# Sparse attention and MoE on one core: the first chunk's attention with scores two units ahead, loads reordered, weights four steps per unit from the first unit on

## The chip, the cores and the metric

The kernel runs on one core of a Trainium2 chip. The metric is the device time of one execution in microseconds (us); of several executions the median is given. The engines are PE (TensorE, matrix products; PEld is its loading of weights), DVE (VectorE), ACT (ScalarE), POOL (GpSimd) and SP (SyncE, which here only issues transfers). Each engine takes its instructions in program order and waits on semaphores. Transfers (DMAs) are issued by SP, ACT and POOL and run on 16 DMA engines.

## What is computed

Block-sparse attention for 4 batches, 8 heads, 768 positions of 64 dimensions, and then a gated two-layer feed-forward network on all 3072 tokens (called MoE in the code):

```python
scores = scale * np.matmul(q, k.transpose(0, 1, 3, 2))
...
mask = np.abs(blk_i - blk_j) <= window
mask = mask | (blk_i == 0) | (blk_j == 0) | (blk_i == n_blocks - 1) | (blk_j == n_blocks - 1)
for qb in range(n_blocks):
    for kb in sampled_blocks[qb]:
        mask[qb * block:(qb + 1) * block, kb * block:(kb + 1) * block] = True
scores = np.where(mask, scores, -1000000000.0)
...
attn = attn / (np.sum(attn, axis=-1, keepdims=True) + 1e-09)
return np.matmul(attn, v).astype(np.float32)
...
h = x @ w_in
g = h * (1.0 / (1.0 + np.exp(-1.702 * h)))
return (g @ w_out).astype(np.float32)
```

A block is 32 positions, so there are 24 blocks. A row of a middle block sees its two neighbours and itself, the first and the last block, and three sampled ones. The first and last block see everything. The network is 512 to 2048 to 512.

## The kernel before

**Units and chunks.** The work is cut into 48 units of 64 tokens: two blocks of one batch, all 8 heads. 44 of them are sparse, 4 dense. Eight units make a chunk of 512 tokens, and there are six chunks. Two sparse units that follow each other belong to two batches and share one entry of K (tiles `kg` and `qt`, loaded by `load_k`, L177) and one of V (tiles `vown` and `vmid`, loaded by `load_v`, L200). There are two buffers of each. An entry of K is 1536 KB (the first ones for a pair of batches 256 KB more), one of V 1280 KB (the first two 1536 KB). `loads()` (L220) issues the next entry of K and then the next of V whenever the entry two before has been used up by the program. SP issues most loads; while `early` is set, POOL issues three of the K loads, and it always issues the two gathers of `vown`.

**One unit of attention.** `scores` (L244): 32 matmuls on PE (L260), then on DVE the negated minima of the scaled, masked scores (`least`, L283) and on ACT the exponentials with their sums (`exps`, L290). `transposes` (L296): eight transposes on PE (L306), two copies from PSUM to `pt` on ACT (L310), and on DVE the reciprocals (`factors`, L345, with L360 and L361). `values` (L315): 64 matmuls on PE (L331), then `normalise` on DVE (L373). `turn` (L379): two transposes on PE (L384), then the split of the result into a high part on ACT (`xhi`, L391) and a low part on DVE (`xlo`, L392). Most of these functions put the PE work into the queue at once and return the ACT and DVE work as a list, so that the caller decides where that goes; `finish` runs such a list. What runs in which order on an engine is just the order in which this code issues it.

**Weights.** `weights()` (L398 on) is a generator that turns the 32 tiles of the two weight matrices, which arrive as 64-bit words, into float32 high and low parts. `fetch` (L414) loads a raw tile of 512 KB from ACT's queue, two tiles ahead, into three buffers. A tile takes four steps, each ended by a `yield`: L446 on DVE; the end of the tile before (`last`, L427 on DVE, and `save`, L433, which stores a w_out tile to DRAM for the later chunks); L452 on DVE and `first` of the next tile (L422 on ACT, which waits for the raw tile); L456 on DVE and the cast L459 on ACT. `first`, L446 and the others work in place in `a`, of which there are three. The list `todo` sets the order of the tiles: in step f the tile f of w_in, and the tile f - 1 of w_out (LAG is 1). A w_out tile from the fourth on (WRING is 3) waits until MoE has used the one three before.

**Order of the first chunk.** `run` (L690) builds indices, calls `loads()`, which issues the first two entries of K and of V in the order K, V, K, V, and then `first()` (L658), written by hand: for each n it issues scores(n) and its minima, two weight steps, turn(n - 2), transposes(n - 1), the exponentials of n, values(n - 1) with normalise, `loads()` and two more weight steps. The first weight step, which fetches the first two raw tiles, comes after the exponentials of unit 0; four weight steps per unit come from n = 2 on, 29 in all. It runs over nine units: the last belongs to the second chunk, and only its scores and exponentials are done here.

**The rest.** Then `tick(m)` (L618) runs 96 MoE steps of 16 per chunk: `up` (L482: L491, L492, L493, into `bank` 7), the gate on ACT and DVE (L499 to L519), `down` (L522: L537, L541, L542). In the first chunk's 16 steps it runs 6 or 9 weight steps in each. The attention of the next chunk is spread over the steps by `plan` (L579), which counts in quarters of a MoE step.

Of the kernel before, what the change touches and what calls it, by code (L numbers as in the profile page):

```python
# [27 lines left out]
NF = DF // P  # L28
NU = (NB - 2) // 2
UT = 2 * BLK  # L30
CU = 8
# [3 lines left out]
RING = 2  # L35
WRING = 3
LAG = 1
# [6 lines left out]
class Kernel:  # L44
# [57 lines left out]
    def indices(self):  # L102
# [7 lines left out]
        def take(shape):  # L110
            n = 1
            for k in shape:
# [8 lines left out]

        vblk = take([NB])
        first, second = slice(1, NB - 2, 2), slice(2, NB - 1, 2)
        nc.gpsimd.iota(vblk[3 * BLK:P, first], pattern=[[2, NU]], base=0, channel_multiplier=0,
                       allow_small_or_imprecise_dtypes=True)
# [118 lines left out]
    def scores(self, g):  # L244
        nc, un, sparse = self.nc, g["unit"], self.sparse(g)
        r = g["k"]["n"] % RING
        g["k"]["scores"] -= 1
        if g["first"]:
            un["rs"] = self.small.tile([P, 2, NPAIR], F32, name="rs")
            un["nm"] = self.small.tile([P, 2, NPAIR], F32, name="nm")  # L250
        sps = self.psum("s", g["n"])
        if sparse:
            bi, n = un["b"] % 2, 2 * P
            kg = self.kg[r][:, :, bi].rearrange("p n (a s) -> p n a s", a=NPAIR)
            for i in range(2):
                for a in range(2):
                    for j in range(2):
                        for h in range(2):
                            pair, rows, c = 2 * i + a, slice(D * h, D * (h + 1)), 2 * a + j
                            nc.tensor.matmul(  # L260
                                sps[h][BLK * c:BLK * (c + 1), n * i:n * (i + 1)].rearrange("p (n s) -> p n s", s=BLK),
                                self.qt[r][rows, bi, UT * pair + BLK * j:UT * pair + BLK * (j + 1)],
                                kg[rows, 4 * j:4 * j + 8, pair], start=True, stop=True, tile_position=(D * h, BLK * c))
            parts = [(i, 0) for i in range(2)]
            bias = self.bias[:, un["u"]].rearrange("p (n o) -> p n o", o=1).broadcast_to([P, 8, BLK])
        else:
            kt = self.kg[r].rearrange("p n b c -> p (n b c)").rearrange("p (a s) -> p a s", a=NPAIR)
            i, half, n = g["i"], g["half"], S // 2
            for a in range(2):
                for h in range(2):  # L270
                    pair, rows = 2 * i + a, slice(D * h, D * (h + 1))
                    nc.tensor.matmul(sps[h][UT * a:UT * (a + 1), 0:n], self.qt[r][rows, 0, UT * pair:UT * (pair + 1)],  # L272
                                     kt[rows, pair, n * half:n * (half + 1)], start=True, stop=True, tile_position=(D * h, UT * a))
            parts = [(i, half)]
            bias = self.zero.broadcast_to([P, n])
        g["ex"] = {}

        def least(h):
            for k, (i, half) in enumerate(parts):
                at = sps[h][:, n * k:n * (k + 1)]  # L280
                if sparse:
                    at = at.rearrange("p (n s) -> p n s", s=BLK)
                nc.vector.tensor_tensor_reduce(out=at, in0=at, in1=bias, scale=-SCALE, scalar=3.0e38, op0=ALU.add, op1=ALU.min,  # L283
                                               accum_out=un["nm"][:, half, 2 * i + h:2 * i + h + 1])

        def exps(h):
            for k, (i, half) in enumerate(parts):
                c = 2 * i + h
                ex = g["ex"][h, k] = self.work.tile([P, 384], F32, name="ex", bufs=4)[:, 0:n]
                nc.scalar.activation(out=ex, in_=sps[h][:, n * k:n * (k + 1)], func=AF.Exp, bias=un["nm"][:, half, c:c + 1],  # L290
                                     scale=-1.0, accum_out=un["rs"][:, half, c:c + 1])

        return [lambda h=h: (least(h), exps(h)) for h in range(2)] if not self.early else [
            lambda: [least(h) for h in range(2)], lambda: [exps(h) for h in range(2)]]
# [103 lines left out]
    def weights(self):  # L398

        nc = self.nc  # L400
        todo = []
        for f in range(NF + LAG):
            if f < NF:
                todo.append((f, 0))
            if f >= LAG:
                todo.append((f - LAG, 1))
        self.ready = set()
        tiles = {}

        def fetch(k):  # L410
            if k < len(todo):
                f, i = todo[k]
                raw = self.work.tile([P, 2 * DM], I32, name="raw", bufs=3)
                nc.scalar.dma_start(out=raw, in_=self.w64[i][f])  # L414
                tiles[k] = {"raw": raw.rearrange("p (a b) -> p a b", b=2)}

        def first(k):


            if k < len(todo):  # L420
                a = tiles[k]["a"] = self.work.tile([P, DM], I32, name="a", bufs=3)
                nc.scalar.activation(out=a.bitcast(F32), in_=tiles[k]["raw"][:, :, 1].bitcast(F32), func=AF.Abs, scale=REBASE)  # L422

        def last(k):
            f, i = todo[k]
            t, w = tiles[k]["t"], tiles[k]["a"].bitcast(F32)
            nc.vector.tensor_tensor(out=t[:, DM:2 * DM], in0=w, in1=t[:, 0:DM].bitcast(F32), op=ALU.subtract)  # L427
            self.ready.add((f, i))

        def save(k):  # L430
            f, i = todo[k]
            if i == 1:
                nc.scalar.dma_start(out=self.ws[f], in_=tiles[k]["a"].bitcast(F32))  # L433
            del tiles[k]

        fetch(0)
        fetch(1)
        yield
        first(0)
        for k, (f, i) in enumerate(todo):  # L440
            while i == 1 and f - WRING > self.downs - 1:
                yield
            fetch(k + 2)
            raw, a = tiles[k]["raw"], tiles[k]["a"]
            low, high = raw[:, :, 0], raw[:, :, 1]
            nc.vector.tensor_scalar(out=a, in0=a, scalar1=3, scalar2=None, op0=ALU.logical_shift_left)  # L446
            yield
            if k > 0:
                last(k - 1)
                save(k - 1)  # L450
                yield
            nc.vector.scalar_tensor_tensor(out=a, in0=high, scalar=-0x80000000, in1=a, op0=ALU.bitwise_and,  # L452
                                           op1=ALU.bitwise_or)
            first(k + 1)
            yield
            nc.vector.scalar_tensor_tensor(out=a, in0=low, scalar=29, in1=a, op0=ALU.logical_shift_right,  # L456
                                           op1=ALU.bitwise_or)
            t = tiles[k]["t"] = self.win[f] if i == 0 else self.wout[f % WRING]
            nc.scalar.copy(out=t[:, 0:DM], in_=a.bitcast(F32))  # L459
            yield  # L460
        last(len(todo) - 1)
        save(len(todo) - 1)
# [155 lines left out]
    def tick(self, m):  # L618
# [16 lines left out]
        after = self.begin(QT * m)  # L635
        finish(after[:3])
        run(n0)
        finish(after[3:])
        if moe:
# [18 lines left out]
    def first(self):  # L658

        items = self.items[:CU + 1]  # L660
        assert items[CU]["unit"]["n"] == CU

        def finish(todo):
            while todo:
                todo.pop(0)()

        def weights(k):
            for _ in range(k):
                next(self.conv)

        for n, g in enumerate(items):
            if n == 1:
                next(self.conv)
            exps = self.scores(g)
            exps.pop(0)()
            if n > 1:
                weights(2)
                finish(self.turn(items[n - 2]))
            if n > 0:
                finish(self.transposes(items[n - 1]))  # L680
            finish(exps)
            if n > 0:
                finish(self.values(items[n - 1]))
            self.loads()
            if n > 1:
                weights(2)
        finish(self.turn(items[CU - 1]))
        self.loads()

    def run(self):  # L690
        self.g, self.wst, self.downs = {}, {}, 0
        self.conv = self.weights()
        self.indices()
        self.loads()
        self.first()
        self.early = False
        self.at = self.plan()
        for m in range(NC * NF + LAG):
            if m == NF:
                for _ in self.conv:  # L700
                    pass
            self.tick(m)
# [50 lines left out]
```

## Time and profile before

| | us |
|---|---|
| median of 3 runs | 782.72 |
| lowest, highest | 781.99, 784.43 |
| the profiled execution | 782.75 |
| its span, first to last instruction | 781.1 |

| engine | busy us | share of the span |
|---|---|---|
| PE | 738.6 | 95% |
| DVE | 412.8 | 53% |
| ACT | 383.5 | 49% |
| POOL | 57.1 | 7% |

The profile gives one execution. A row of the instructions in order of time has the start in us from the start of the span, the duration in us, engine, line, operation, what it writes and reads, the shapes and a count of instructions merged into it; in square brackets stands how long the engine was idle before it, and what ended that. ACTq, SPq and POOLq are the issue of transfers. Matmuls overlap, so PE's busy time is not PE at its peak. A transfer row tells of its issue alone.

### The profile page before, as it was taken

Reading aid. Unit: us, or ns where it says so; the run is one execution under the profiler, and the core shown is the slowest. Engines: PE = TensorE matmul, PEld = TensorE weight load, DVE = VectorE, ACT = ScalarE, POOL = GpSimd, SP = SyncE. Lnnn points to the kernel's source line nnn. Section 1 sums busy time; section 2 is a strip of 40 time slices with the busy share of each in tenths; the row PEclk is TensorE's granted clock in tenths of the full one; section 3 lists DMA queues with packets and bytes.
Section 4 is the critical chain, followed back from the end, with each engine's and each line's share of the span. In section 5 each row is a group of like instructions: output and inputs, shape, how many; then the busy total and the mean of one; then the engine's idle time right before and its main releaser. Section 6 shows DMA issues by size and latency. Waiting matters only on the chain.

```text
span 781.1 us, 19264 instructions
## 1 busy us (share of the span) xinstructions
PE 738.6 (95%) x7584; PEld 571.7 (73%) x7584; DVE 412.8 (53%) x1076; ACT 383.5 (49%) x950; POOL 57.1 (7%) x85
## 2 busy tenths in 40 slices
PE   2667999999999999999999999999999999999996
PEld 1445787767777777787877877877777777888884
DVE  3387779887644354445445544444554444443332
ACT  1567667666545444444444544444545454333332
POOL 5122001101000001000000000000000000000000
PEclk9699999999999999999999999999999999999998
DMA  8998887786644437664534465435574321041112
GB/s 267 281 367 296 251 254 256 251 259 222 206 162 153 117 114 219 173 177 129 161 117 145 142 175 156 137 115 163 161 229 153 93 98 42 28 108 40 55 41 55
DMA packets 61117, 128.22 MB, mean 164 GB/s; under 512 B 7569, under 2 KB 26514, under 8 KB 60514
## 3 DMA queue, kind: packets, MB, share of 16 engines
q1 hardware_dynamic: 46882, 80.50, 33.9%
q0 software_dynamic: 7232, 25.51, 10.1%
q10 hardware_dynamic: 6912, 20.97, 8.1%
q8 instruction: 60, 0.98, 0.5%
q14 instruction: 31, 0.25, 0.1%
HBM read 116.47 MB, written 10.49 MB: 163 GB/s over the span
## 4 chain that ended last, share of the span: by engine, by line
PE 78%; DMA 7%; DVE 7%; ACT 4%; issue 2%; SPq 1%; ACTq 0%; DVEq 0%
PE bank L491 11%; PE bank L541 10%; PE bank L542 10%; PE bank L537 10%; PE bank L493 10%; PE bank L492 10%; PE bank L260 5%; PE bank L306 4%; PE bank L331 4%; DMA ws<-a 3%; DMA kg<-in_kb_dram 2%; PE bank L339 2%; PE bank L272 2%; DMA raw<-in_moe_w_in_dram 2%; DVE a L452 1%
## 5 line engine op out<-in xcount | busy, mean ns | idle before, releaser
L491 PE MATMUL bank<-xhi,win 128*128 128x512 f32 x384 | 158.4, 412 | 1.2 <-ACT xhi L391 0.9
L290 ACT ACTIVATE ex<-bank,nm 128x256 f32<-128x256 f32 (+1 forms) x208 | 99.7, 492 | 115.4 <-DVE nm L283 113.6
L506 DVE SCALAR_TENSOR_TENSOR g<-g,bank 128x512 f32<-128x512 f32 x83 | 57.1, 687 | 183.8 <-ACT g L499 183.8
L541 PE MATMUL bank<-wout,ghi 128*128 128x512 f32 x384 | 154.1, 401 | 0.0
L542 PE MATMUL bank<-wout,ghi 128*128 128x512 f32 x384 | 151.7, 395 | 0.0
L493 PE MATMUL bank<-xhi,win 128*128 128x512 f32 x384 | 151.0, 393 | 0.0
L492 PE MATMUL bank<-xlo,win 128*128 128x512 f32 x384 | 150.0, 391 | 0.0
L499 ACT ACTIVATE g<-bank 128x512 f32<-128x512 f32 x96 | 57.5, 599 | 146.4 <-PE bank L493 146.1
L537 PE MATMUL bank<-wout,glo 128*128 128x512 f32 x384 | 107.7, 394 | 0.0
L480 DVE TENSOR_TENSOR wout<-wst,wout 128x512 fp32r<-128x512 f32 x80 | 55.4, 693 | 79.7 <-ACT wout L479 78.7
L511 ACT CAST ghi<-g 128x512 fp32r<-128x512 f32 x96 | 59.7, 622 | 54.6 <-DVE g L506 54.6
L491 PEld LDWEIGHTS bank<-xhi,win 128*128 128x128 f32 x384 | 72.1, 188 | 18.7 <-ACT xhi L391 1.1
L537 PEld LDWEIGHTS bank<-wout,glo 128*128 128x128 f32 x384 | 72.4, 189 | 17.3
L493 PEld LDWEIGHTS bank<-xhi,win 128*128 128x128 f32 x384 | 72.1, 188 | 16.3
L283 DVE CUSTOM_DVE_ANT_1 bank<-bank,bias 128x256 f32<-128x256 f32 x176 | 73.8, 440 | 19.3 <-PE bank L260 16.2
L542 PEld LDWEIGHTS bank<-wout,ghi 128*128 128x128 f32 x384 | 72.5, 189 | 15.6
L541 PEld LDWEIGHTS bank<-wout,ghi 128*128 128x128 f32 x384 | 72.2, 188 | 16.0
L492 PEld LDWEIGHTS bank<-xlo,win 128*128 128x128 f32 x384 | 72.3, 188 | 13.3 <-DVE xlo L392 0.3
L216 POOL DMA_INDIRECT vown<-in_v_dram,vidx x44 | 43.7, 994 | 496.9 <-PE bank L331 385.5
L260 PE MATMUL bank<-kg,qt 64*32 64x256 f32 x1408 | 55.8, 416 | 17.6 <-DMA vmid<-in_v_dram 10.5
L310 ACT COPY pt<-bank 128x512 f32<-128x512 f32 (+1 forms) x120 | 61.1, 563 | 19.4 <-PE bank L306 19.3
L331 PEld LDWEIGHTS bank<-vown,pt 128*32 128x32 f32 x1408 | 43.8, 113 | 31.8 <-ACT pt L310 16.0
(75 smaller groups left out, 821.8 us busy)
## 6 DMA issues: line engine op xcount, KB each, us to landing
wst<-ws SPq DMA_DIRECT2D x80, 256.0 KB, 2.7
kg<-in_kb_dram SPq DMA_DIRECT2D x136, 128.0 KB, 3.2
kg<-in_kb_dram SPq DMA_DIRECT2D x22, 384.0 KB, 4.9
raw<-in_moe_w_in_dram ACTq DMA_DIRECT2D x16, 512.0 KB, 9.7
raw<-in_moe_w_out_dram ACTq DMA_DIRECT2D x16, 512.0 KB, 4.5
kg<-in_kT_dram SPq DMA_DIRECT2D x4, 1536.0 KB
vown<-in_vd_dram SPq DMA_DIRECT2D x8, 768.0 KB, 6.0
qt<-in_q_dram SPq DMA_DIRECT2D x22, 256.0 KB, 4.9
```

The lines of the kernel that those rows point to most:

```text
L260: nc.tensor.matmul(sps[h][BLK * c:BLK * (c + 1), n * i:n * (i + 1)].rearrange("p (n s) -> p n s", s=BLK), self.qt[r][rows, bi, UT * pair + ...
L283: nc.vector.tensor_tensor_reduce(out=at, in0=at, in1=bias, scale=-SCALE, scalar=3.0e38, op0=ALU.add, op1=ALU.min, accum_out=un["nm"][:, ha ...
L290: nc.scalar.activation(out=ex, in_=sps[h][:, n * k:n * (k + 1)], func=AF.Exp, bias=un["nm"][:, half, c:c + 1], scale=-1.0, accum_out=un["r ...
L310: copies.append(lambda pt=pt, ps=ps, m=m: nc.scalar.copy(out=pt[:, 0:m], in_=ps[:, 0:m]))
L331: nc.tensor.matmul(av[BLK * c:BLK * (c + 1), 0, 2 * i + h], g["pt"][h][:, 2 * i + k, BLK * c:BLK * (c + 1)], src[:, at:at + D], start=(k = ...
L491: nc.tensor.matmul(h, wih[:, k], hi[:, k], start=(k == 0), stop=False)
L492: nc.tensor.matmul(h, wih[:, k], lo[:, k], start=False, stop=False)
L493: nc.tensor.matmul(h, wil[:, k], hi[:, k], start=False, stop=(k == NCT - 1))
L511: self.nc.scalar.copy(out=ghi, in_=self.g[m][0])
L537: nc.tensor.matmul(o[n], glo[:, tk[n]], woh, start=False, stop=last)
L541: nc.tensor.matmul(o[n], ghi[:, tk[n]], woh, start=(f == 0), stop=False)
L542: nc.tensor.matmul(o[n], ghi[:, tk[n]], wol, start=False, stop=False)
```

## The change

It has four parts.

1. The order in the first chunk. Scores and minima of units 0 and 1 come first, then `loads()`, the exponentials of unit 0 and the first weight step. Then for each unit n of the eight: transposes(n) with the copies and the factors, turn(n - 1) with xhi and xlo, scores(n + 2) with its minima, the exponentials of n + 1, the matmuls of values(n), `loads()`, two weight steps, normalise(n), and two more weight steps. For the last unit the two before normalise are put behind it.
2. Weight steps: four from unit 0 on, 33 in all.
3. `run` issues the first two entries of K and one of V; the second entry of V comes with the first `loads()`, behind the third entry of K.
4. The order of the weight tiles: the w_out tiles from the fourth on come one step f later, behind one more w_in tile.

```diff
@@ weights()
         todo = []
-        for f in range(NF + LAG):
+        lag = lambda f: LAG if f < WRING else LAG + 1
+        for f in range(NF + LAG + 1):
             if f < NF:
                 todo.append((f, 0))
-            if f >= LAG:
-                todo.append((f - LAG, 1))
+            todo += [(k, 1) for k in range(NF) if k + lag(k) == f]
@@ first()
-        for n, g in enumerate(items):
-            if n == 1:
-                next(self.conv)
-            exps = self.scores(g)
-            exps.pop(0)()
-            if n > 1:
+        exps = {}
+
+        def scores(n):
+            if n < len(items):
+                exps[n] = self.scores(items[n])
+                exps[n].pop(0)()
+
+        for n in range(2):
+            scores(n)
+        self.loads()
+        finish(exps[0])
+        next(self.conv)
+        for n in range(CU):
+            todo = self.transposes(items[n])
+            if n > 0:
+                todo += self.turn(items[n - 1])
+            finish(todo)
+            scores(n + 2)
+            finish(exps[n + 1])
+            todo = self.values(items[n])
+            self.loads()
+            if n < CU - 1:
                 weights(2)
-                finish(self.turn(items[n - 2]))
-            if n > 0:
-                finish(self.transposes(items[n - 1]))
-            finish(exps)
-            if n > 0:
-                finish(self.values(items[n - 1]))
-            self.loads()
-            if n > 1:
-                weights(2)
+            finish(todo)
+            weights(2 if n < CU - 1 else 4)
         finish(self.turn(items[CU - 1]))
         self.loads()
@@ run()
-        self.loads()
+        for e in self.kent[:RING]:
+            self.load_k(e)
+        self.load_v(self.vent[0])
+        self.knext, self.vnext = RING, 1
         self.first()
```

## The prediction

> **What bounds the kernel now.** The profiled run took 782.75 us, 1.65 us more than its span, and the median of the runs before is 782.72 us, so the profiled execution stands for the median and sums against it need no correction. I read the page first, then the busy time by stages.
>
> ```profile
> span 781.1 us, 19264 instructions
> ```
>
> ```profile
> 10.00:75.00 65.00, 42.63 (x889) 28.32 (x889) 40.66 (x140) 38.07 (x114) 19.94 (x27) 0.84 0.95 320
> 23.00:30.00 7.00, 4.24 (x54) 2.91 (x44) 2.28 (x9) 0.55 (x4) 0.00 (x0) 0.60 1.03 279
> 59.00:63.00 4.00, 3.81 (x97) 2.30 (x98) 1.73 (x6) 3.09 (x11) 1.43 (x2) 0.57 0.29 107
> 75.00:165.00 90.00, 88.34 (x924) 68.16 (x923) 75.45 (x176) 61.84 (x142) 7.01 (x6) 1.00 0.80 255
> 165.00:200.00 35.00, 34.29 (x446) 26.20 (x446) 26.10 (x70) 22.29 (x56) 2.34 (x2) 1.00 0.70 219
> ```
>
> The columns after the stretch are its length, the busy time of PE, PEld, DVE, ACT and POOL, the granted clock, the DMA share and GB/s. The change touches the first stretch: eight units of attention before the first MoE matmul. There no engine is full, the DMA engines nearly are (0.95), and PE is busy 42.63 of 65 us. After 75 us PE is never idle long, so whatever the first stretch gains or loses is carried to the end almost unchanged: the later order of work is counted in quarters of MoE steps, not in time. So the question is when the first L491 starts. Next I read ACT and DVE in order of time.
>
> ```profile
> 18.84 0.38 ACTq L414 DMA_DIRECT2D raw<-in_moe_w_in_dram  x1
> ...
> 30.23 0.66 ACT L422 ACTIVATE a<-raw 128x512 f32<-128x512 f32 x1 [6.68 <-DMA raw<-in_moe_w_in_dram]
> ...
> 32.16 0.66 ACT L422 ACTIVATE a<-raw 128x512 f32<-128x512 f32 x1 [1.26 <-DMA raw<-in_moe_w_in_dram]
> ...
> 42.45 0.62 ACT L459 CAST win<-a 128x512 fp32r<-128x512 f32 x1 [0.48 <-DVE a L456]
> ...
> 42.98 0.67 ACT L422 ACTIVATE a<-raw 128x512 f32<-128x512 f32 x1
> ...
> 43.80 1.08 ACT L310 COPY pt<-bank 128x512 f32<-128x512 f32 x2
> 44.75 0.50 ACT L290 ACTIVATE ex<-bank,nm 128x256 f32<-128x256 f32 x1
> ...
> 57.71 0.69 ACT L422 ACTIVATE a<-raw 128x512 f32<-128x512 f32 x1 [2.85 <-DMA ws<-a]
> ...
> 73.05 0.62 ACT L459 CAST wout<-a 128x512 fp32r<-128x512 f32 x1 [0.27 <-DVE a L456]
> ...
> 74.24 0.37 ACT L391 CAST xhi<-bank 128x256 fp32r<-128x256 f32 x1 [0.57 <-DMA kg<-in_kb_dram]
> ```
>
> ```profile
> 30.93 0.43 DVE L446 TENSOR_SCALAR a<-a 128x512 int32<-128x512 int32 x1 [1.40 <-ACT a L422]
> 31.42 0.69 DVE L452 SCALAR_TENSOR_TENSOR a<-raw,a 128x512 int32<-128x512 int32 x1
> ...
> 37.59 0.43 DVE L283 CUSTOM_DVE_ANT_1 bank<-bank,bias 128x256 f32<-128x256 f32 x1 [0.53 <-PE bank L260]
> ...
> 42.67 0.42 DVE L283 CUSTOM_DVE_ANT_1 bank<-bank,bias 128x256 f32<-128x256 f32 x1
> ...
> 44.44 0.69 DVE L427 TENSOR_TENSOR win<-a,win 128x512 fp32r<-128x512 f32 x1
> 45.05 0.68 DVE L452 SCALAR_TENSOR_TENSOR a<-raw,a 128x512 int32<-128x512 int32 x1
> 45.65 0.42 DVE L392 TENSOR_TENSOR xlo<-bank,xhi 128x256 fp32r<-128x256 f32 x1
> 45.98 0.20 DVE L360 TENSOR_SCALAR rg<-rs 128x4 f32<-128x4 f32 x1
> ...
> 46.50 0.42 DVE L373 TENSOR_TENSOR x<-bank,ri 128x256 f32<-128x256 f32 x1
> 46.84 0.68 DVE L456 SCALAR_TENSOR_TENSOR a<-raw,a 128x512 int32<-128x512 int32 x1
> 47.44 0.42 DVE L446 TENSOR_SCALAR a<-a 128x512 int32<-128x512 int32 x1
> ...
> 63.12 0.43 DVE L283 CUSTOM_DVE_ANT_1 bank<-bank,bias 128x256 f32<-128x256 f32 x1 [0.47 <-PE bank L260]
> ...
> 68.19 0.43 DVE L283 CUSTOM_DVE_ANT_1 bank<-bank,bias 128x256 f32<-128x256 f32 x1
> 72.33 0.68 DVE L456 SCALAR_TENSOR_TENSOR a<-raw,a 128x512 int32<-128x512 int32 x1
> 74.65 0.42 DVE L392 TENSOR_TENSOR xlo<-bank,xhi 128x256 fp32r<-128x256 f32 x1 [1.30 <-ACT xhi L391]
> ```
>
> Three things are to be seen. ACT, which takes its work in order, stands 6.68 us in front of the first weight tile, fetched at 18.84 and there at 30.23; behind it wait DVE (L446) and all later attention. From unit 3 on, one round runs from one L283 to the next: 5.07 us at its best (63.12 to 68.19), where DVE has no gap, and (68.19 - 37.59)/5 = 6.12 us on average, because ACT waits for transfers (2.85 us at 57.71). And the last round hands over fast: last L456 at 72.33, xhi at 74.24.
>
> ```profile
> 59.20 2.00 PE bank L331 x64
> 61.19 1.81 PE bank L260 x32
> ...
> 74.67 0.50 PE bank L491
> ```
>
> **The change, part by part. The new round.** Scores two units ahead take the score matmuls off the path: they are done a whole round before their exponentials. But the new order of one unit is, on DVE, factors, xlo of the unit before, minima of the unit after next, L427, L452, normalise, L456, L446; on ACT it is pt, xhi, exponentials, L422, L459. In the old order xlo stood behind L427 and L452, and ACT had those 3 us to get xhi done. Now the two copies pt and the cast xhi stand behind L459, L459 waits for L456, and xlo leads DVE's next round. That closes a loop: L456 to L459 0.72 (72.33 to 73.05), L459 0.53 (42.45 to 42.98), both pt 0.95 (43.80 to 44.75), xhi to xlo 0.41 (74.24 to 74.65), xlo 0.33 (45.65 to 45.98), minima 1.77 (42.67 to 44.44), L427 0.61, L452 0.60, normalise 0.34, and L456 again: 6.26 us. That is above the old best of 5.07 and next to the old mean of 6.12. What it buys is cover: ACT works only about 4 us of that round, so L422 stands some 2 us before L459 is due, and waits like the 2.85 at 57.71 mostly vanish in it. I take 6.26 for each of five rounds, 31.3 us against 30.6, and up to 1 us more in all for waits that are too long for the cover.
>
> PE is not the bound even at its slow pace: transposes 1.72 (row below), scores 1.81, values 2.00, and two more transposes at a quarter of the 1.72 make 6.0 us, just inside 6.26.
>
> ```profile
> 19.38 1.72 PE L306 MATMUL bank<-ident,ex 128*128 128x128 f32 x8 [1.46 <-ACT ex L290]
> ```
>
> **From the first weight tile to the rounds.** Call its arrival at ACT L0. From L422 to L446 0.70 (30.23 to 30.93), L446 0.49, L452 0.60, normalise 0.34, then L456 to L459 0.72, and 0.53, 0.95, 0.41, 0.33 as in the loop: the minima of unit 3 start at L0 + 5.07. The second tile came 1.93 us after the first and is covered up to 2.3. Before, it was L0 + 7.36. Here two units of lead gain 2.3 us.
>
> **The end of the stretch.** Minima of unit 8 at L0 + 36.4, its L456 at + 3.32 = L0 + 39.7. Then comes a unit without scores: L459 and pt 2.20, values up to 2.00 (I take 1.8), normalise 0.34, and only then four weight steps instead of two: L427 and L452 1.21, L456 to L459 0.72, xhi 1.19 behind that (73.05 to 74.24) and L491 0.43 later: about 7.9 us, where the old end took 2.34 from its last L456. So the first L491 starts at L0 + 47.6. Before it was 30.23 + 44.44. The new order needs 3.2 us more after the first tile, and makes one more tile of weights in it.
>
> **Loads.** Before, both entries of V were issued ahead of the weights:
>
> ```profile
> 13.91 1.74 SPq L212 DMA_DIRECT2D vmid<-in_v_dram  x2
> ```
>
> ```profile
> 14.46 0.99 POOL L216 DMA_INDIRECT vown<-in_v_dram,vidx  x1 [0.30 <-issue]
> ...
> 18.28 0.58 POOL L198 DMA_DIRECT2D kg<-in_kb_dram  x1 [1.56 <-PE bank L260]
> 19.48 0.57 POOL L198 DMA_DIRECT2D kg<-in_kb_dram  x1 [0.62 <-issue]
> ```
>
> Now the second entry of V (1536 KB: three transfers of SP, two of POOL) goes behind the third of K, which waits for the scores at 18.28, so the raw tiles, issued at the same 18.84, meet 1.57 MB less. At 279 to 320 GB/s that is 4.9 to 5.6 us of DMA time. Bounds for L0: 5.6 us earlier, if all of it had stood ahead of the tile; no earlier, if three queues share the engines evenly and the tile's part stays a third, since that V entry then comes back beside it from about 22 us. I take 3 us, near the middle, since the third of K needs POOL until about 21 us and until then the tile has little beside it: L0 = 27.2. The first V entry moves behind the second K entry, on POOL behind three issues of 1.2 us (18.28 to 19.48). Its user, the values of unit 0, has cover until its normalise, which waits for L0 in any case. The second K entry comes earlier; it is needed for the scores of unit 2, which now have the whole wait before L0 as cover. Without that cover they would cost their 1.81 on PE.
>
> **Weights.** 33 steps instead of 29 come before MoE. The four are worth 0.60 + 0.42 + 0.61 + 0.60 = 2.2 us of DVE (L456, L446, L427, L452 above). The new order of tiles (w_out one later from the fourth on) keeps the rate, since the ring of w_out still holds the conversion to the MoE steps, so the four fall out at the end, in 165 to 200 us, where PE is busy 34.29 of 35 and DVE 26.10. Bounds: nothing, or all 2.2. I take 0.7.
>
> **Sum.** L491 at 27.2 + 47.6 = 74.8 against 74.67: 0.1 later; 0.7 back at the end; 782.75 + 0.1 - 0.7 = 782.2 us. A change under 0.3% (2.35 us) can't be told from none here.
>
> **The rivals. Slower, 785.4 us: the weights still come at 30.2.** The loop and the longer end then cost their 3.2 us, less 0.7 at the end, and with none to little of the 1 us for waits: 782.75 + 3.2 - 0.7 = 785.3, or 785.4 with a tenth of it. It decides once L0 is later than about 29.7. For it speaks that the tile took 11.4 us for 1 MB (two raws) while the engines ran at 279 GB/s, which is a third of that rate. Against it, that in 18 to 22 us fewer packets compete. The Trainium skill, "DMA: Bandwidth & Descriptors", section "Queues, rings and completion order", states that each DMA engine takes turns between the queues that have work, packet by packet; by that rule the third stays a third, and this rival would hold. The 92 GB/s of the two raws agree with it as far as they go, while no run here shows the new mix.
>
> **Faster, 778.9 us: the weights come at 24.6.** Then L491 is at 72.2, 2.5 earlier, and with 1.4 of the 2.2 at the end 782.75 - 2.5 - 1.4 = 778.9. For it: the new loads leave ACT's queue nearly alone until 22 us. Against it: the engines still move the same bytes by about 33 us. A second way to it is that DMA, idle for most of 59 to 63 us (0.29), fills that hole with loads that are now issued sooner; but loads that come sooner do not shorten a 6.26 us loop.
>
> **The lead does nothing, 782.7 us:** ACT is blocked before the first tile as before, and if the rounds stay at 6.1 because transfers still set them, the 2.3 us won after L0 go to the longer end. That lies inside the forecast and has its chance there.
>
> **How the numbers follow.** The forecast, within 0.3%, has 0.48. The faster rival has 0.30, because both its terms lie inside the bounds and I may have the loop too long by what ACT and DVE overlap; the slower has 0.22. The range runs from the faster rival with the other 0.8 of the weights' bound and 0.6 off the five rounds (777.5) to the slower with next to nothing back at the end (786.0). Between them, the forecast's own range is 780.4 to 785.1.
>
> **What would show it.** Right: first L422 near 27 us; minima every 6.2 to 6.4 us with DVE idle about 1.2 us before xlo ("<-ACT xhi"), and no DVE wait on PE there; first L491 near 75; fewer ACT waits on DMA in 33 to 70 us. Wrong: rounds near 5.1 us, or L422 before 25 us (faster); L422 after 30 or rounds over 6.8 us (slower).

## The result, and the profile after

The changed kernel takes 789.06 us (median of 8 runs, 786.58 to 792.35), the kernel before 784.09 us beside it (median of 8, 781.99 to 785.74). The ratio is 1.0063, with a 95% interval of 1.0041 to 1.0085: the change makes the kernel 0.63% slower. That is above the range that was forecast. The profiled execution took 788.95 us and can stand for the median. The one of the kernel before (782.75) lies 1.3 us below the median that its runs have here, so the two profiles are 6.2 us apart where the medians are 5.0 apart; what follows accounts for the 6.2.

First the span, and busy time by stretch; columns as in the prediction.

```profile
span 787.3 us, 19242 instructions
```

```profile
10.00:75.00 65.00, 41.84 (x838) 25.68 (x842) 39.33 (x137) 35.33 (x104) 18.36 (x25) 0.86 0.98 315
23.00:30.00 7.00, 3.33 (x76) 2.30 (x75) 3.91 (x12) 1.73 (x8) 0.97 (x1) 0.92 1.04 396
75.00:80.00 5.00, 3.98 (x60) 3.34 (x55) 3.34 (x7) 3.64 (x13) 2.15 (x2) 0.50 0.95 284
80.00:85.00 5.00, 5.00 (x36) 3.59 (x44) 2.29 (x6) 2.37 (x5) 0.00 (x0) 0.65 0.65 243
```

Up to 75 us both kernels move about the same number of bytes (315 GB/s now, 320 before), but the changed one has done 51 PE instructions less by then (838 against 889), and is not yet at its first MoE matmul. Between 75 and 82.5 us PE runs at the clock 0.50, where the kernel before had 1.00.

The instructions of ACT in order of time show where the first stretch went.

```profile
26.98 0.66 ACT L422 ACTIVATE a<-raw 128x512 f32<-128x512 f32 x1 [2.96 <-DMA raw<-in_moe_w_in_dram]
...
29.95 0.67 ACT L422 ACTIVATE a<-raw 128x512 f32<-128x512 f32 x1 [2.31 <-DMA raw<-in_moe_w_in_dram]
29.96 0.33 ACTq L414 DMA_DIRECT2D raw<-in_moe_w_in_dram  x1
...
36.77 0.62 ACT L459 CAST win<-a 128x512 fp32r<-128x512 f32 x1
39.49 0.34 ACTq L414 DMA_DIRECT2D raw<-in_moe_w_out_dram  x1
39.92 1.07 ACT L310 COPY pt<-bank 128x512 f32<-128x512 f32 x2 [2.53 <-DMA raw<-in_moe_w_in_dram]
...
52.22 0.62 ACT L459 CAST win<-a 128x512 fp32r<-128x512 f32 x1 [2.00 <-DVE a L456]
53.69 0.33 ACTq L414 DMA_DIRECT2D raw<-in_moe_w_out_dram  x1
54.12 1.07 ACT L310 COPY pt<-bank 128x512 f32<-128x512 f32 x2 [1.28 <-issue]
...
59.87 0.62 ACT L459 CAST wout<-a 128x512 fp32r<-128x512 f32 x1 [2.02 <-DVE a L456]
59.93 0.33 ACTq L414 DMA_DIRECT2D raw<-in_moe_w_in_dram  x1
60.40 1.06 ACT L310 COPY pt<-bank 128x512 f32<-128x512 f32 x2
```

The first weight tile arrives at 26.98, as forecast. Then look between L459 and the copies `pt`. At 59.87 they follow one another at once. At 36.77 the cast is over at 37.39, but ACT goes on only at 39.49, with a fetch (L414), and the copies come 2.53 us late "<-DMA raw". Nothing that the copies read comes from that transfer: it is the fetch in front of them that waited. At 52.22 the same gap is 1.28 us.

On DVE, one row of each round:

```profile
32.74 0.42 DVE L283 CUSTOM_DVE_ANT_1 bank<-bank,bias 128x256 f32<-128x256 f32 x1
41.30 0.42 DVE L392 TENSOR_TENSOR xlo<-bank,xhi 128x256 fp32r<-128x256 f32 x1 [3.85 <-ACT xhi L391]
41.64 0.42 DVE L283 CUSTOM_DVE_ANT_1 bank<-bank,bias 128x256 f32<-128x256 f32 x1
...
48.19 0.42 DVE L283 CUSTOM_DVE_ANT_1 bank<-bank,bias 128x256 f32<-128x256 f32 x1
55.51 0.42 DVE L392 TENSOR_TENSOR xlo<-bank,xhi 128x256 fp32r<-128x256 f32 x1 [2.58 <-ACT xhi L391]
55.85 0.42 DVE L283 CUSTOM_DVE_ANT_1 bank<-bank,bias 128x256 f32<-128x256 f32 x1
61.77 0.42 DVE L392 TENSOR_TENSOR xlo<-bank,xhi 128x256 fp32r<-128x256 f32 x1 [1.30 <-ACT xhi L391]
62.11 0.42 DVE L283 CUSTOM_DVE_ANT_1 bank<-bank,bias 128x256 f32<-128x256 f32 x1
...
69.16 0.42 DVE L283 CUSTOM_DVE_ANT_1 bank<-bank,bias 128x256 f32<-128x256 f32 x1
```

From the minima of unit 3 (32.74) to those of unit 8 (69.16) are 36.42 us: rounds of 8.90, 6.55, 7.66, 6.26 and 7.05, mean 7.28. The fourth is exactly the loop of 6.26. What the others have over it (2.64, 0.29, 1.40, 0 and 0.79, together 5.1) stands almost whole as added wait of `xlo` for `xhi`: 3.85 and 2.58, for example, where the loop alone has 1.30. Those waits are ACT's at L414 passed on: the fetch starts 0.06 us behind L459 in the fourth round, and 2.66, 0.31, 1.41 and 0.80 later than that in the others.

The last part is the chain of waits around the first MoE step.

```profile
74.34 2.00 PE bank L331 x64
...
76.91 0.69 PE bank L384 x2
77.60 1.72 PE bank L306 x8
79.36 0.36 ACT xhi L391
79.76 0.79 PE bank L491
...
81.01 0.43 PE bank L493
...
83.57 0.24 PE bank L493
...
84.53 0.60 ACT g L499
```

The first L491 starts at 79.76, where 74.8 was forecast and the kernel before had 74.67. Until 83.57 its matmuls follow one another every 0.43 us instead of every 0.23, so that the gate L499 comes 4.77 us after it; before, it was 3.28 (74.67 to 77.95). So 5.09 us are lost up to L491 and 1.49 in the first step. By the twelfth step the difference is 6.08, and it is 6.2 in the span.

### The profile page after: what moved, and what is told of

Its sections match the earlier page's. It is cut to its first block, busy times and chain, and to the rows that moved or that the text cites. A ratio compares the mean times of both kernels' runs of the same rounds, so it can differ in the third digit from the quotient of the medians.

```text
span 787.3 us, 19242 instructions
## 1 busy us (share of the span) xinstructions
PE 743.0 (94%) x7584; PEld 573.6 (73%) x7584; DVE 412.5 (52%) x1076; ACT 382.8 (49%) x950; POOL 56.6 (7%) x85
## 4 chain that ended last, share of the span: by engine, by line
PE 77%; DVE 9%; DMA 5%; ACT 5%; issue 2%; SPq 1%; ACTq 1%; DVEq 0%
PE bank L491 11%; PE bank L541 10%; PE bank L542 10%; PE bank L493 10%; PE bank L537 10%; PE bank L492 10%; PE bank L306 5%; PE bank L331 4%; PE bank L260 4%; DMA raw<-in_moe_w_in_dram 2%; DMA ws<-a 2%; PE bank L339 2%; PE bank L272 2%; DVE bank L283 2%; DVE a L452 1%
## 5 line engine op out<-in xcount | busy, mean ns | idle before, releaser
L491 PE MATMUL bank<-xhi,win 128*128 128x512 f32 x384 | 159.2, 414 | 0.8 <-ACT xhi L391 0.5
L499 ACT ACTIVATE g<-bank 128x512 f32<-128x512 f32 x96 | 57.5, 599 | 147.5 <-PE bank L493 147.5
L491 PEld LDWEIGHTS bank<-xhi,win 128*128 128x128 f32 x384 | 72.5, 189 | 18.6 <-ACT xhi L391 0.9
L493 PEld LDWEIGHTS bank<-xhi,win 128*128 128x128 f32 x384 | 72.5, 189 | 16.5
L542 PEld LDWEIGHTS bank<-wout,ghi 128*128 128x128 f32 x384 | 72.5, 189 | 15.6
L519 DVE TENSOR_TENSOR glo<-g,ghi 128x512 fp32r<-128x512 f32 x96 | 65.8, 685 | 2.1 <-ACT ghi L511 2.1
```

The lines of the kernel that those rows point to most:

```text
L491: nc.tensor.matmul(h, wih[:, k], hi[:, k], start=(k == 0), stop=False)
L493: nc.tensor.matmul(h, wil[:, k], hi[:, k], start=False, stop=(k == NCT - 1))
L519: self.nc.vector.tensor_tensor(out=glo, in0=g, in1=ghi.bitcast(F32), op=ALU.subtract)
L542: nc.tensor.matmul(o[n], ghi[:, tk[n]], wol, start=False, stop=False)
```

## The experiments

Two theories were put against each other. In the first, A, the order of ACT's work is at fault: the fetch stands inside the loop, and every wait there is passed on to the attention in full. In the second, B, the supply is: the weights start earlier, the DMA engines are full, and some instruction or other must wait for the bytes, wherever the fetch stands. The table has all runs. Each ratio is to the kernel before in runs on the same chip, with its 95% interval; "median" is of the runs of that kernel. The other columns come from the one profiled execution: first L422, minima of unit 3, mean of the five rounds from there, first L491, all in us. The medians of the kernel before were 784.09 (the result), 784.56 (the first four rows below), 784.86 (the next four) and 787.15 (the last four).

| kernel | ratio | median | L422 | unit 3 | round | L491 |
|---|---|---|---|---|---|---|
| before (profiled: 782.75) | 1 | 784.09 | 30.23 | 37.59 | 6.12 | 74.67 |
| after | 1.0063 (1.0041 to 1.0085) | 789.06 | 26.98 | 32.74 | 7.28 | 79.76 |
| e1_fetch_after_exps | 1.0008 (0.9990 to 1.0025) | 785.97 | 25.74 | 32.33 | 6.65 | 76.64 |
| e2_loads_only | 0.9990 (0.9970 to 1.0009) | 783.70 | 26.91 | 37.85 | 6.68 | 77.04 |
| e3_xlo_behind_L452 | 1.0020 (0.9997 to 1.0043) | 786.70 | 27.59 | 32.01 | 6.88 | 77.07 |
| e4_29_steps | 1.0029 (1.0015 to 1.0043) | 786.55 | 29.14 | 36.17 | 7.14 | 81.65 |
| e5_after_light | 1.0022 (0.9999 to 1.0046) | 785.93 | 26.93 | 32.38 | 6.59 | 75.87 |
| e6_before_light | 0.9957 (0.9939 to 0.9976) | 782.04 | 30.35 | 39.03 | 5.58 | 73.63 |
| e7_fetch_and_xlo | 1.0005 (0.9981 to 1.0029) | 785.50 | 27.01 | 32.51 | 6.02 | 75.06 |
| e8_both_29_steps | 0.9983 (0.9963 to 1.0003) | 784.10 | 26.67 | 31.18 | 6.90 | 75.83 |
| e9_weights_from_unit1 | 0.9973 (0.9954 to 0.9993) | 785.23 | 29.45 | 28.14 | 7.44 | 75.96 |
| e10_both_25_steps | 0.9925 (0.9896 to 0.9955) | 781.75 | 29.52 | 28.17 | 7.17 | 73.76 |
| e11_both_21_steps | 0.9932 (0.9905 to 0.9959) | 782.14 | 33.45 | 27.96 | 7.08 | 73.16 |
| e12_before_25_steps | 0.9929 (0.9909 to 0.9950) | 781.02 | 31.74 | 32.08 | 6.52 | 71.03 |

Executions of one kernel differ by some us (786.58 to 792.35 for the changed one), so a profile's L491 is one draw, and the ratios carry the verdicts.

**The fetch out of the loop.** The changed kernel with the fetch issued behind the exponentials, a step later:

```diff
-            fetch(k + 2)
+            late = self.early or fetch(k + 2)
...
-            yield
+            yield; late and fetch(k + 2)
```

> The changed kernel, with the fetch of the next raw tile moved on ACT from between L459 and the copies pt to behind the exponentials of the same round. Theory A (the fetch waits on ACT for an earlier transfer, and what waits behind it is pt, in the loop of the round): the five rounds take 6.3 to 6.5 us each where the changed kernel has 7.28, the first L491 starts near 75 to 76 us instead of 79.75, and the run takes 784 to 785.5 us. Theory B (the transfers' supply sets the rounds, wherever the waits stand): rounds stay at 7.0 to 7.3 us, the waits show up at L422 instead, L491 near 79, and 788 to 789 us.

Measured: 1.0008, so 0.55% of the 0.63% come back, and L491 3.1 us earlier. But not every wait is gone. Part of them has moved to L422, as ACT's rows in order of time show:

```profile
42.61 0.69 ACT L422 ACTIVATE a<-raw 128x512 f32<-128x512 f32 x1 [2.55 <-DMA raw<-in_moe_w_in_dram]
...
56.55 0.66 ACT L422 ACTIVATE a<-raw 128x512 f32<-128x512 f32 x1 [3.41 <-DMA ws<-a]
...
69.52 0.66 ACT L422 ACTIVATE a<-raw 128x512 f32<-128x512 f32 x1 [2.46 <-DMA ws<-a]
```

The first of these waits for a raw tile, the other two for the store of an older tile (`ws`) out of the buffer `a` that L422 is to write. L422 has some 2 us of cover, and the rounds are 6.65 instead of 7.28; three of the five are 6.26 or 6.27. The place of the fetch matters (A), and the transfers are still late (B).

**The loads alone.** The kernel before with the new order of its first loads and nothing else (the `loads()` at the end of a round moves into the branch for n > 0, so that the first round has none):

```diff
-            self.loads()
+                self.loads()
...
-        self.loads()
+        for e in self.kent[:RING]:
+            self.load_k(e)
+        self.load_v(self.vent[0])
+        self.knext, self.vnext = RING, 1
```

> The kernel before, with the new order of the first loads alone (second entry of V behind the third of K). Theory A: the first weight tile comes at 27 us as in the changed kernel, the old rounds of 5.1 to 6.1 us follow, the first L491 starts near 72 to 73 us, and the run takes 780.5 to 782 us against about 784 for the kernel before. Theory B: the same bytes have to come by the same time, so L491 stays at 74 to 75 us and the time within 1 us of the kernel before.

```profile
26.91 0.68 ACT L422 ACTIVATE a<-raw 128x512 f32<-128x512 f32 x1 [2.43 <-DMA raw<-in_moe_w_in_dram]
31.25 0.66 ACT L422 ACTIVATE a<-raw 128x512 f32<-128x512 f32 x1 [3.67 <-DMA raw<-in_moe_w_in_dram]
```

The first tile comes 3.3 us earlier than before (26.91 against 30.23), just as in the changed kernel, and it is worth nothing: 0.9990 with 1 in the interval. ACT waits 3.67 us for the second tile instead, which comes at 31.25, only 0.9 us sooner than before (32.16), and the minima of unit 3 (37.85) are where they were (37.59). That speaks for B: the same bytes come by nearly the same time.

**Another way out of the loop.** The changed kernel, with `xlo` behind L452 as in the old order, `xhi` where it was:

```diff
-        return [copies]
+        return [high, low] if early else [lambda: (high(), low())]
...
-                todo += self.turn(items[n - 1])
+                high, *low = self.turn(items[n - 1])
+                todo.append(high)
...
-            finish(todo)
+            finish(low + todo)
```

> The changed kernel with xlo of the unit before put on DVE behind L452 instead of ahead of the minima, so that DVE does not stand still for L459, fetch, pt and xhi. Theory A: rounds of 5.8 to 6.4 us, since the fetch still waits in front of pt but about 1.2 us of it are now beside DVE's work; L491 near 74 to 76 us; 783 to 785.5 us. Theory B: 7.0 to 7.3 us a round, and 788 to 789 us.

Measured: 1.0020; 0.43% come back, and rounds are 6.88. The loop through `xlo` is open here, but the fetch is still ahead of `pt`. Each of e1 and e3 takes away most of the loss: the wait hurts because both are there, a fetch that waits and a loop that passes its wait on.

**Fewer steps at the end.** The changed kernel with 29 steps and the old order of the tiles:

```diff
-        lag = lambda f: LAG if f < WRING else LAG + 1
+        lag = lambda f: LAG
...
-            weights(2 if n < CU - 1 else 4)
+            weights(2 if n < CU - 1 else 0)
```

> The changed kernel with 29 weight steps ahead of MoE instead of 33 (none behind the last normalise) and the old order of the weight tiles. Both theories leave the rounds at about 7.3 us. The end gets shorter by the four steps: from L456 of unit 6 to the first L491 5.0 to 5.8 us instead of 7.3, so L491 near 77.5 to 78. If the four steps cost as much later in the MoE steps, the run takes 788 to 789 us; if they find room there, as 74 of 90 us of DVE suggest, 786 to 787 us.

Measured: 1.0029, half of the loss back. Its profiled execution, 789.96, is the longest of its ten and not typical, so its L491 decides nothing. The four steps that the change adds ahead of MoE, with their order of tiles, thus cost some 0.3% net, though they give time back later; the intervals just touch (1.0015 to 1.0043, 1.0041 to 1.0085), so the size is uncertain.

**The supply taken away.** The changed kernel and the kernel before, each with light raw tiles from the fourth on while the first chunk lasts; all instructions stay:

```diff
-                nc.scalar.dma_start(out=raw, in_=self.w64[i][f])
+                n = 128 if self.early and k >= 3 else 2 * DM; nc.scalar.dma_start(out=raw[:, 0:n], in_=self.w64[i][f][:, 0:n])
```

> The changed kernel in which the raw tiles from the fourth on, while the first chunk runs, are fetched with an eighth of their bytes (64 of 512 words a row, repeated when read); so those weights are left out and the output is not the reference's. Every instruction and every issue stays. It takes 3.2 to 3.6 MB out of what the transfers must bring between 27 and 80 us. Theory A (the order of the round, 6.26 us, is the floor, and the supply adds the rest): rounds of 6.3 to 6.5 us. Theory B (supply alone): rounds of 5.1 to 5.7 us, as in the light kernel before.

> The kernel before with the same light fetches from the fourth raw tile on; it leaves out the same weights. Theory A: rounds of 5.1 to 5.4 us (DVE's work of a round), so about 1.1 us less a round than the light changed kernel, and the first L491 near 70 us. Theory B: the same 5.1 to 5.7 us as the light changed kernel.

DVE's rows of the changed order with light tiles:

```profile
46.54 0.42 DVE L283 CUSTOM_DVE_ANT_1 bank<-bank,bias 128x256 f32<-128x256 f32 x1
...
59.08 0.42 DVE L283 CUSTOM_DVE_ANT_1 bank<-bank,bias 128x256 f32<-128x256 f32 x1
...
65.00 0.42 DVE L392 TENSOR_TENSOR xlo<-bank,xhi 128x256 fp32r<-128x256 f32 x1 [1.29 <-ACT xhi L391]
65.34 0.42 DVE L283 CUSTOM_DVE_ANT_1 bank<-bank,bias 128x256 f32<-128x256 f32 x1
```

From 46.54 on the rounds are 6.27, 6.27 and 6.26: the loop of 6.26, shown by itself. The old order with light tiles:

```profile
50.44 0.43 DVE L283 CUSTOM_DVE_ANT_1 bank<-bank,bias 128x256 f32<-128x256 f32 x1 [1.14 <-PE bank L306]
...
55.51 0.42 DVE L283 CUSTOM_DVE_ANT_1 bank<-bank,bias 128x256 f32<-128x256 f32 x1
...
61.87 0.43 DVE L283 CUSTOM_DVE_ANT_1 bank<-bank,bias 128x256 f32<-128x256 f32 x1 [1.21 <-PE bank L306]
...
66.94 0.42 DVE L283 CUSTOM_DVE_ANT_1 bank<-bank,bias 128x256 f32<-128x256 f32 x1
```

Its rounds change between 5.07 and 6.36, since in every second one DVE waits for PE; the mean is 5.58. So the new order costs 0.7 us per round by itself (6.26 for 5.58); in the means of the table it is 1.0, since the first two rounds of the new order (7.61 and 6.55) still wait. And by the ratios the bytes of the raw tiles cost both orders about the same: 0.41% in the new one (1.0063 to 1.0022), 0.43% in the old (1 to 0.9957), each known to some 0.2 or 0.3%. The single profiles differ more: L491 comes 3.9 us earlier with light tiles in the new order and 1.0 in the old. This is the plainest answer to the prediction: the runs show nothing that the cover of the lead of two units hides and the old order did not hide.

**Both moves.** The changed kernel with the edits of e1 and e3, and then with that of e4 too:

```diff
+            late = self.early or fetch(k + 2)
...
+            yield; late and fetch(k + 2)
...
+            finish(low + todo)
```

> The changed kernel with both moves: the fetch behind the exponentials, and xlo behind L452. The loop of 6.26 us is open and only the supply is left. Theory A: rounds of 6.0 to 6.4 us, first L491 at 74 to 76 us, and a ratio to the kernel before of 0.997 to 1.001. Theory B (the moves only shift waits): like the move of the fetch alone, rounds of 6.6 and a ratio of 1.000 to 1.002.

```diff
+        lag = lambda f: LAG
...
+            weights(2 if n < CU - 1 else 0)
```

> The same two moves, and 29 weight steps with the old order of the weight tiles. In the changed kernel the four steps left out gave 0.34%. Theory A: the end of the stretch is 1.5 to 2.5 us shorter, L491 at 72 to 74.5 us, ratio 0.995 to 0.999, below the kernel before. Theory B (the four steps cost the same wherever they stand once the rounds are in order): ratio within 0.001 of the kernel with the two moves alone.

Measured: 1.0005 and 0.9983. Mended like this the order is as fast as the old one and no faster, though the rounds of e7 are down to 6.02 and L422 is at 27.0. The two moves do not add up (e1 alone has 1.0008). What is left these runs do not settle: the supply, and in the profile of e7 also PE's clock, since its first MoE step takes 5.12 us from L491 to L499 instead of 3.28.

**The weights' start.** The changed kernel with the weight steps from unit 1 on, and nothing else changed; 29 steps are left, four of them at the end:

```diff
-            if n < CU - 1:
+            if 0 < n < CU - 1:
                 weights(2)
...
-            weights(2 if n < CU - 1 else 4)
+            weights(0 if n < 1 else 2 if n < CU - 1 else 4)
```

> The changed kernel without weight steps in unit 0: they run from unit 1 on, 29 in all, with the four at the end and the new tile order kept. Theory A (the order of the round and the fetch in it make the loss; the wait of ACT before the first tile holds everything behind it): pt and the exponentials of units 1 and 2 no longer wait for the first tile, the minima of unit 3 start near 28 us instead of 32.7, rounds stay at 6.3 to 7.3 us, L491 at 75 to 78 us, 785.5 to 788 us. Theory B (the supply alone): one tile less has to come, 0.5 MB or about 1.5 us; 787 to 788 us, with longer rounds after the earlier start.

Measured: 0.9973. In this comparison the kernel before had a higher median than in the others (787.15), so the sign against it is less sure than the interval says; against the changed kernel the gain is 0.9% by the ratios and 3.8 us by the medians. It has two parts that this run does not separate, the later start and four steps less; e4, with the same 29 steps, gained 0.34%. ACT's rows show that its long wait is at another place, once:

```profile
37.44 0.34 ACTq L414 DMA_DIRECT2D raw<-in_moe_w_in_dram  x1
37.82 1.07 ACT L310 COPY pt<-bank 128x512 f32<-128x512 f32 x2 [4.18 <-DMA vmid<-in_v_dram]
```

Here the fetch, and with it `pt`, waited for a load of V by SP, whose data neither of them touches. It does not always hit `pt`: in e10 (below) the fetch stands ahead of L422 and waits longer still, for a load of Q by SP:

```profile
43.69 0.68 ACT L422 ACTIVATE a<-raw 128x512 f32<-128x512 f32 x1 [7.07 <-DMA qt<-in_q_dram]
```

In e9, after that round (11.4 us) the others are 7.01, 6.28, 6.26 and 6.27.

**Fewer weights ahead of MoE.** Both moves with 25 steps, from unit 1 on (e10), and with 21, from unit 2 on (e11); and the kernel before with 25 steps, from n = 3 on (e12):

```diff
-            if n < CU - 1:
+            if 0 < n < CU - 1:
                 weights(2)
-            finish(todo)
-            weights(2 if n < CU - 1 else 4)
+            finish(low + todo)
+            weights(0 if n < 1 else 2 if n < CU - 1 else 0)
```

> Both moves (fetch behind the exponentials, xlo behind L452), weight steps from unit 1 on, none behind the last normalise: 25 steps, old tile order. The kernel with 29 steps had a ratio of 0.9983. Theory A: the minima of unit 3 start near 28 us, rounds of 6.0 to 6.5 us, L491 at 70 to 73 us; the first two MoE steps, which run out of weight steps in the kernel before, take the missing four for up to 1 us; ratio 0.994 to 0.997. Theory B: the supply holds the rounds at 6.5 to 7 us after the earlier start, L491 at 73 to 75, ratio 0.997 to 0.999.

```diff
+            if 1 < n < CU - 1:
                 weights(2)
...
+            weights(0 if n < 2 else 2 if n < CU - 1 else 0)
```

> The same from unit 2 on, 21 steps. Theory A: the first tile is there when ACT comes to it, L491 at 68 to 72 us, but the first MoE steps have to make up eight steps; ratio 0.993 to 0.998. Theory B: as much better than with 25 steps as 0.5 MB less is worth, about 1.5 us, and the same again given back in the MoE steps; ratio 0.996 to 0.999.

```diff
-            if n > 1:
+            if n > 2:
                 weights(2)
+            if n > 1:
                 finish(self.turn(items[n - 2]))
...
-            if n > 1:
+            if n > 2:
                 weights(2)
```

> The kernel before, with its weight steps from n = 3 on instead of n = 2: 25 steps, nothing else. Theory A: ACT reaches the first tile after the exponentials of unit 2, so pt and xhi do not wait for it; the minima of unit 3 come 2 to 4 us sooner; L491 at 71 to 73.5 us; ratio 0.995 to 0.999. If it gains as much as the kernel with the two moves and 25 steps, then the lead of two units brings nothing of its own. Theory B: 0.5 MB less, 0.998 to 1.000.

Measured: 0.9925, 0.9932 and 0.9929. These three beat both kernels, also by their medians (781.0 to 782.1, where the kernel before has 784.1 to 787.2 in the four comparisons). They are alike within their intervals: with equally few steps the old order does as well as the mended lead of two units. Of e12, the stretch up to MoE and two rows of ACT:

```profile
10.00:75.00 65.00, 43.96 (x932) 29.98 (x932) 41.63 (x143) 39.15 (x116) 19.94 (x27) 0.92 1.00 333
```

```profile
31.74 1.25 ACT L422 ACTIVATE a<-raw 128x512 f32<-128x512 f32 x2
33.12 1.11 ACT L310 COPY pt<-bank 128x512 f32<-128x512 f32 x2
```

ACT no longer stands in front of the first tile: both tiles are there when it comes to them at 31.74, and the minima of unit 3 come at 32.08 instead of 37.59. PE does 932 instructions by 75 us, against 889 before and 838 in the changed kernel. How much of the gain is ACT's wait and how much the fewer bytes before MoE, these runs do not tell apart.

## Why the prediction was wrong, point by point

**The first weight tile: right.** 26.98 for 27.2. The slower rival, in which the tile stays at 30.2, did not happen, though a slower result came out: what made it slower was something else. But 27.2 was chosen between bounds of 24.6 and 30.2, so that it came so close is in part luck. Beside the rival stood the rule of the Trainium skill, "DMA: Bandwidth & Descriptors", "Queues, rings and completion order", that each engine takes turns between the queues with work. What was inferred from it, that the tile keeps its third and its time, does not hold here. The share held roughly, the rate did not: from 23 to 30 us the engines moved 396 GB/s instead of 279 at nearly the same busy share (1.04 and 1.03), and the two raw tiles (1.05 MB) took 10.6 us (19.32 to 29.95), by estimate a quarter of the 396. The prediction had counted both of them as there at 30.23; the second came at 32.16, so before they took 13.3 us, 28% of the 279. Why the engines moved more is not shown; the second entry of V was in that stretch too, its gathers issued at 22.00 and 23.29.

**From the first tile to unit 3: 0.7 too low.** 5.76 for 5.07. The second tile came 2.97 us after the first, not 1.93, and the cover there is 2.3.

**The loop: right, as a floor.** 6.26 was forecast, and 6.26 to 6.27 is what four rounds without a wait have (one in the changed kernel, three each in e1 and e5; e9 has three of 6.26 to 6.28). PE is no bound there, as said.

**The waits in the rounds: this is the step that failed.** The prediction said that waits like the 2.85 at 57.71 "mostly vanish" in the cover, and allowed "up to 1 us more in all", of which its sum took nothing: the 47.6 us from the first tile to L491 have no term for waits. Measured are 5.1 us over five loops. The cover was real, but it lies ahead of L459, for L422. The fetch of the tile after next stands behind L459, on the same engine, with `pt`, `xhi` and by `xlo` the next round behind it, and there is no cover at all. In the part on what is moved, the fetch was not counted among the instructions of its step that can wait. In the kernel before it waits too (0.7 us at 54.96, behind the L459 of 54.24); but there `save` and L422 are next, not `pt`.

What it waits for can be read from the program as compiled. This is ACT's queue in the changed kernel, with the counters that each instruction waits on in brackets:

```
L459 CAST win_102<-a 128x512 [waits DVE_49]
L414 DMA raw<-in_moe_w_out_dram 128x1024 [waits DMAHW6_49,Activation_49]
L310 COPY pt<-bank_88 128x512 [waits PE_49,Activation_49]
L310 COPY pt<-bank_92 128x512 [waits PE_49,Activation_49]
L391 CAST xhi_120<-bank_91 128x4x64 [waits PE_49]
...
L414 DMA raw<-in_moe_w_in_dram 128x1024 [waits DMAHW7_49,Activation_49]
...
L414 DMA raw<-in_moe_w_out_dram 128x1024 [waits DMAHW0_49,Activation_49]
```

In this program the transfers of SP and ACT share eight completion counters, DMAHW0 to DMAHW7, in turn. An issue waits until the transfer that had its counter last has landed, whatever it carried. The first L414 of the list, the fetch at 39.49, waits so for the raw tile fetched at 29.96; the third, the fetch at 53.69, for a load of Q that SP issued; in e9 the fetch at 37.44 waits for a load of V. That the wait goes through the counter is read from the compiled programs and from these rows; no run changed the counters alone. That the fetch's place in the loop makes its wait cost what it does is shown by e1 (0.55% back) and e3 (0.43% back); that it is transfers that are waited for, by e5 (0.41% back).

**The end of the stretch: 0.6 too high.** 7.29 from the last L456 to L491, for 7.9.

**The clock in the first MoE step: not foreseen, 1.5 us.** In the last unit PE has no scores to compute. First the busy time by stretch there, then the kernel before, then PE's two longest pauses in order of time:

```profile
70.00:72.50 2.50, 1.07 (x6) 0.40 (x4) 2.47 (x10) 1.17 (x5) 0.00 (x0) 1.00 1.03 364
72.50:75.00 2.50, 1.09 (x26) 0.79 (x30) 1.25 (x5) 1.81 (x5) 0.00 (x0) 0.64 0.97 261
80.00:82.50 2.50, 2.50 (x6) 1.86 (x7) 2.29 (x6) 1.38 (x4) 0.00 (x0) 0.50 0.98 354
```

```profile
67.50:70.00 2.50, 1.21 (x10) 0.97 (x10) 2.43 (x11) 1.58 (x4) 0.00 (x0) 1.00 1.04 412
70.00:72.50 2.50, 1.34 (x65) 1.02 (x65) 2.36 (x9) 2.50 (x9) 0.45 (x1) 1.00 1.05 395
```

```profile
72.61 0.44 PE L384 MATMUL bank<-ident,x 128*128 128x128 f32 x2 [1.51 <-DVE x L373]
74.34 0.31 PE L331 MATMUL bank<-vown,pt 128*32 128x64 f32 x1 [1.30 <-ACT pt L310]
```

From 70 to 75 us PE of the changed kernel is busy 2.16 us. The granted clock falls, and the first matmuls of MoE follow every 0.43 instead of 0.23 us. The Trainium skill, "TensorE: Matmul & The Clock Gate", "What's actually happening", has two states, half and full rate, with the full one after about 3.4 us of sustained work. The trace agrees with it in the factor (0.43 to 0.23) and roughly in the time (L491 at 79.76, fast from 83.57 on: 3.8 us; counted from L384 at 76.91, with one pause of 0.45 us, it would be 6.7). The same section of the Trainium skill puts the fall to half rate behind an idle window of 3.4 us; here the longest pause was 1.51 us, so by the trace thin work is enough. How thin is not settled: the kernel before, busy 2.55 us of the 5 from 67.5 to 72.5, kept 1.00. Nor was this term tried by itself; it differs between the runs (3.28 us from L491 to L499 in the kernel before, 3.33 in e5 and 3.01 to 3.29 in e10 to e12, but 4.31 in e8, 4.96 in e9, 5.12 in e7 and 6.14 in e3), so the ratios of the experiments may hold a part of it too.

**The four steps: 0.5 back for 0.7.** Near in size, but not in place: it came back between the sixth and the eleventh step (114 to 152 us), not at 165 to 200, and no run shows that it was the four steps. They also lengthen the stretch at its most exposed place (e4).

The account: 74.8 forecast for L491, less 0.2 for the tile, plus 0.7, plus 5.1, less 0.6, makes 79.8, and 79.76 was measured. With 1.5 for the clock and 0.5 given back, 6.1 of the span's 6.2 us are found. The list of signs named the one that came true, rounds over 6.8 us, but the rivals had no mechanism for it.

## What to carry to other kernels

When a step is moved on an in-order engine, write down for each of its instructions, the issue of a transfer included, what it can wait for, and what stands directly behind it in the new place; cover ahead of one of them is none for the next. Before weights or other loads are started earlier, look at whether the transfers are full: here an earlier start moved no more bytes by 75 us (315 GB/s, 320 before) and gained nothing, and a later start with fewer steps ahead of MoE (e12) was worth 0.7% in its comparison (0.4% against 784.09, the lowest of the four medians of the kernel before).

## What the runs showed of the hardware that was not expected

A transfer's issue can hold its engine for microseconds because of transfers that another engine issued: 4.18 us at 37.82 in e9, where ACT's fetch waited for a load of V issued by SP, and 7.07 us at 43.69 in e10, for a load of Q. The DMA engines show a share of 1.03 to 1.04 both at 279 GB/s and at 396 GB/s, so that a full share does not say how much they move. And PE's clock fell with no pause over 1.51 us, from thin work alone, and stayed at half for 3.8 us of the unbroken work that followed.
